# One attention tile moves from the second half of a gated FFN kernel to its attention stage, the rest start one chunk later, and the transfers at the change of halves are placed in another order

## The chip, the cores and the metric

The kernel runs on one core of a Trainium2 chip. The metric is device time in microseconds (us), the median of several executions. A profile, taken by the hardware profiler on one further execution, shows what each engine did: PE (TensorE, matrix products; its weight loads are listed as PEld), DVE (VectorE), ACT (ScalarE), POOL (GpSimd) and SP (SyncE, which here issues every transfer between the chip's memory and the on-chip buffers).

## What is computed

For 2048 tokens `x` of width 576 (all in float32):

```python
xn = layernorm(x)
q, k, v = split(xn @ wqkv)             # 32 heads of 18
pq, pk = phi(q), phi(k)                # phi(t) = (t + 1 if t > 0 else exp(t)) + 1e-6
kv = einsum("hsd,hse->hde", pk, v);  z = sum_s pk
o  = (pq @ kv) / (pq . z + 1e-6)       # linear attention, no softmax
s  = o @ wo
h  = gelu(xn @ w1 + b1)                # 576 -> 4608
g  = silu(h @ w2 + b2)                 # 4608 -> 576
out = x + s * g
```

## The kernel before, in words

Every float32 operand of a matrix product is split into a high and a low part, and a product is three matrix instructions (high by high, high by low, low by high). The two large products of the FFN are made with a seven-product scheme for 2 by 2 blocks of a matrix; the products of one block are numbered 1 to 7, and in the second matrix product they run in the order 1, 2, 7, 4, 5, 3, 6 (`ORDER`).

The work has four stages.

1. **Projections.** `q`, `k`, `v` of 16 token tiles of 128, the state `kv` and the sums `z`. Some tiles of `q` are written to the chip's memory (`q_dram`).
2. **Attention stage** (from `fold_wo` to `ordered.close()`). The masked state is folded with `wo` into five blocks `kw`, each split into high and low (`split_kw`, line 1191) and also stored (`store_kw`, line 1196, tensor `kw_dram`). Then, for each tile in the list `TO` (line 1065, nine tiles), GpSimd multiplies `q` by the sums (`by_sums`, line 1099, tile `bs`), VectorE makes the denominators (`denominators`, line 1106, tile `den`), GpSimd divides (`p_mult`, line 1114, tiles `vb` and `pbuf`, three buffers), ScalarE fills a pad (`pad`), TensorE transposes five blocks (`transpose_p`, line 1248; line 1252 in the profile, tile `ptp`), ScalarE and VectorE split the result (`th`, `tl`, lines 1256 to 1258), and TensorE makes 28 products into `ps_s` (`attend_mm`, line 1287). The result goes to `s_dram`. All engines' instructions here, SP's too, stay in the order of the program text (`in_order()`). `load_q(j)` (line 1178) reads a tile of `q` back; four buffers hold such tiles, and one becomes free when `p_mult` has read it.
3. **FFN in two halves of eight tiles**, 18 chunks of the loop at line 2050, numbered 0 to 17 here (`step` in the code; `c` counts within a half, so chunk 9 is `c == 0` of the second half). A chunk is 14 products of the first matrix product (profile line 1569, outputs `a`, `b`, `zy`, `e`, seven instructions each), then 14 half-products of the second one (line 1731, output `pm`, twelve instructions each). Around these, everything else is hung on a plan: `add(place, function)` puts work at one of 28 places of a chunk (`NS = 28`; places 0 to 13 are the first matrix product, 14 to 27 the second), and `at_step` writes it out there. The instructions of PE, DVE, ACT and POOL keep that order; the order on SP's queue is not fixed by hand. In the first half the split operands of `w1` and `w2` are made and stored; in the second half they are read back: `load_we` (line 1338, tile `we`), `W1Loaded` (line 1407, tiles `wa`, `wc`, `wd`), `load_six` (line 1420, `we<-op` in the profile), and `W2.load` (line 1658, tiles `w__...`, three buffers in turn, so that product 4's operand takes the buffer of product 1's).
4. **Tail**: chunk 17 without the seven-product scheme, and the last eight tiles of output.

At the change of halves, between chunks 8 and 9, the first half's four sums (`C11`, `C22`, `C21`, `C12`) are passed through silu and stored by `store_first` (line 1809, `c_dram<-macc`), to be gated and written out tile by tile in chunks 10 to 17. The tiles of attention that are not in `TO` (`LATER_TILES`, tiles 0 to 6) are done in the second half, one per chunk, by the class `Attention` (line 1927): its folded blocks come from `kw_dram` (`load_block`, `split_folded`, tile `kw`), the sums from `zb_dram` into `b2b` (`load_sums`), a tile of `q` into `qa`; the stations of one tile are in the table `A_AT`, by place relative to the next chunk (`load` 8 places ahead, `sums` 1 ahead, `transpose` at 4, `product` at 6). So a tile planned in chunk n is multiplied in chunk n + 1; tile 0 is planned in chunk 9.

```python
    A_AT = dict(
        load=-8, phi=-5, phi_max=-4, sums=-1, denominators=1, scale=1, pad=2, banks=3, transpose=4,
        operands=4, product=6, store=7,
    )
    W2_NEXT = {1: 24, 2: 26, 7: 27, 4: 44, 5: 46, 3: 48, 6: 50}
```

Of the kernel before, what the change touches and what calls it, by code (L numbers as in the profile page):

```python
# [30 lines left out]
NC = NF // CF  # L31
# [4 lines left out]
QH = 4  # L36
# [11 lines left out]
def linear_attention_gated_ffn(ctx, tc, x, xT, wqkv, wo, w1, w1e, b1, w2, b2, out):  # L48
# [804 lines left out]
    late = {}  # L853
# [206 lines left out]
    for p in range(2, NPR):  # L1060
# [3 lines left out]

    TO = [
        2 * NPR - 3, 2 * NPR - 4, 2 * QH, 2 * QH + 1, 2 * NPR - 2, 2 * QH + 2, 2 * NPR - 1,
        2 * QH + 3, 2 * QH - 1,
    ]
    NA = len(TO)
    kvz, sums_k, last_row, zb_first = (late[n] for n in ("kvz", "sums_k", "last_row", "zb"))  # L1070
# [120 lines left out]
    def split_kw(k, elo):  # L1191
        h, l = (w[k] for w in kw_ops)
        nc.scalar.copy(h, krs[k])
        elo.tensor_tensor(l, krs[k], h.bitcast(F32), op=SUB)
# [33 lines left out]
    def load_x_pair(q, p):  # L1228
        nc.sync.dma_start(X[:, q].bitcast(F32), x_dram[p])
# [18 lines left out]
    def transpose_p(j):  # L1248
        pb = p_bufs[j % len(p_bufs)]
        pt = bank2(f"ptp{j}").rearrange("p a b -> p (a b)")  # L1250
        for k in range(KT):
            nc.tensor.transpose(pt[:, k * P : (k + 1) * P], pb[:, k * P : (k + 1) * P], ident)
        th = thp.tile([P, KT, P], F32R, tag="th", name=f"th{j}")
        tl = thp.tile([P, KT - 1, P], F32R, tag="tl", name=f"tl{j}")
        p3 = pt[:, : KT * P].rearrange("p (k c) -> p k c", k=KT)
        nc.scalar.copy(th, p3)
        nc.vector.tensor_tensor(tl, p3[:, :4, :], th[:, :4, :].bitcast(F32), op=SUB)
        nc.vector.tensor_tensor(th[64:, 4, :], p3[64:, 4, :], th[64:, 4, :].bitcast(F32), op=SUB)
        pT[j] = (th, tl)

    split_kw(3, dve)
    store_kw(3)
    transpose_p(0)
    split_kw(4, dve)
    store_kw(4)
    load_x_pair(2, QH)
# [242 lines left out]
    for j in range(NA):  # L1509
        attend(j)  # L1510
        if j + 2 < NA:
            transpose_p(j + 2)
        if j + 3 < NA:
            pad(j + 3)
        if j == 0:
            phi_q_hi(TO[6])
        if j == 1:
            phi_q_max(TO[6])
        if j + 5 < NA:
            by_sums(j + 5)  # L1520
        if j + 4 < NA:
            denominators(j + 4)
            p_mult(j + 4)
        if j == 0:
            load_q(8)
            load_x_pair(3, QH + 1)
        beside(j)
    ordered.close()
    ph2.close()
# [11 lines left out]
    C11, C12, C21, C22, U1 = range(5)  # L1541
# [348 lines left out]
    NS = 28  # L1890
# [159 lines left out]
    for step in range(n_chunks):  # L2050
        half, c = divmod(step, NC)
        base = step * NS
        plain = step == n_chunks - 1
        h = HOps(c)
        if half == 1 and c == 0:
            a = Attention(None)
            add(base + 20, a.folded_places)
            add(base + 26, a.load_sums)
            for k in range(KT):
                add(base + 20 + k, a.load_block, k)  # L2060
                add(base + 26 + k, a.split_folded, k)
        if half == 1 and c < len(LATER_TILES):
            a = Attention(LATER_TILES[c])
            for what, at in A_AT.items():
                if what not in ("phi", "phi_max") or a.t < 4:
                    late = c == 0 and what in ("sums", "denominators", "scale", "pad")
                    add(base + NS + at + late, getattr(a, what))
        if half == 0:
            plan_w1(add, w1t[2 * step + 1], base, **P1)
            add(base, w2t[step].sum7)  # L2070
            for k in range(2):
                add(base + 2, w2t[step].sum4, k)
            for i, (at, lo) in PW2.items():
                add(base + at, w2t[step].hi, i)
                add(base + lo, w2t[step].lo, i)
            if (c, 5) not in w2_dram:
                w = w2t[step]
                for i, (at, hi, lo) in W2_SUMS_HERE.items():
                    add(base + at, w.sum5 if i == 5 else w.sum6)
                    add(base + hi, w.hi, i)  # L2080
                    add(base + lo, w.lo, i)
        change = step == NC - 1
        if not plain:
            add(base + (11 if change else 7), load_we, 2 * step + 2)
            add(base + (16 if change else 14), load_we, 2 * step + 3)
        if half == 0 and c < NC - 1:
            add(base + 0, make, W1, w1t, 2 * step + 2)
            add(base + 4, make, W1, w1t, 2 * step + 3)
            add(base + 1, lambda n=2 * step + 2, base=base: plan_w1(add, w1t[n], base, **P0))
            make(W2, w2t, step + 1)  # L2090
            add(base + 22, w2t[step + 1].load_raw)
            if (c + 1, 5) in w2_dram:
                for i, at in W2_SUMS_NEXT.items():
                    add(base + at, lambda i=i, n=step + 1: w2t[n].load(i))
        elif not plain:
            at = (11, 11, 16) if change else (7, 14, 24) if step == NC else (7, 14, 14)
            add(base + at[0], make, W1Loaded, w1t, 2 * step + 2)
            add(base + at[1], load_six, 2 * step + 2)
            add(base + at[2], make, W1Loaded, w1t, 2 * step + 3)
            if step + 2 < n_chunks:  # L2100
                make(W2, w2t, step + 1)
                for i, at in W2_NEXT.items():
                    add(base + max(at, 28 * change), lambda i=i, n=step + 1: w2t[n].load(i))
            else:
                make(W2, w2t, step + 1)

                w = w2t[step + 1]
                add(base + 13, w.load_raw)
                for f in range(CF):
                    add(base + 22 + f, lambda f=f, w=w: (w.plain(f), w.hi(("p", f))))  # L2110
                    add(base + 24 + f, w.lo, ("p", f))
        if not plain:
            if half == 0 and c == NC - 1:
                for k, at in X_AT.items():
                    add(base + at, load_x_next, k)
                add(base + 25, silu_first, C11)
                for k in range(2):
                    add(base + 26 + k, combine, C12, nc.vector, slice(2 * k, 2 * k + 2))
                    add(base + 26 + k, combine, C21, nc.gpsimd, slice(2 * k, 2 * k + 2))
            for what in ("S", "hi", "lo"):  # L2120
                for (i, pr), at in PH[what].items():
                    add(base + at, getattr(h, what), i, pr)
        if half == 1 and c == 0:
            add(base, silu_first, C12)
            add(base, silu_first, C21)
            add(base, combine, C22, nc.vector, slice(0, 2))
            add(base + 1, combine, C22, nc.vector, slice(2, 4))
            add(base + 1, silu_first, C22)
            for k, m in enumerate((C11, C22, C21, C12)):
                add(base + 5 + 2 * k, store_first, m)  # L2130
        if half == 1 and c:
            for k in range(2):
                tiles = {}
                def load(k=k, t=c - 1, tiles=tiles):
                    tiles[0] = finish_tiles(k)
                    finish_load(t, k, tiles[0])
                add(base, load)
                add(base + 4, lambda k=k, t=c - 1, tiles=tiles: finish(t, k, tiles[0]))
        if plain:
            for m in (C12, C21, C22):  # L2140
                add(base + 4, combine, m, nc.gpsimd)
            for t, at in enumerate((6, 7, 12, 13, 5, 13, 13, 13)):
                add(base + at, load_xs, t)
            for b, f, at, lo in (
                (0, 0, 7, 8), (0, 1, 8, 9), (1, 0, 10, 10), (1, 1, 10, 11), (0, 2, 11, 12),
                (0, 3, 12, 13), (1, 3, 13, 13), (1, 2, 13, 13),
            ):
                add(base + at, tail_split, b, f)
                add(base + lo, tail_lo, b, f)
        for j in range(CF // 2):  # L2150
            n = 2 * step + j
            u = Up(n, w1t.pop(n), xs)
            for k, i in enumerate(UP):
                u.step(i)
                h.add(j, u.g)
                at_step(base + 7 * j + k)
        if plain:
            break
        held = {}
        for k, i in enumerate(ORDER):  # L2160
            for q2 in (0, 2):
                product(c, i, q2, [h.ops[i, 0], h.ops[i, 1]], w2t[step].ops[i], held)
                at_step(base + 14 + 2 * k + q2 // 2)
        if change:
            second_half()
# [60 lines left out]
```

## Time and profile before

| | us |
|---|---|
| median of 3 runs | 1109.28 (1109.06 to 1110.73) |
| the profiled execution | 1107.14 |
| its span, first to last instruction | 1105.3 |

| engine | busy us | share of the span |
|---|---|---|
| PE | 1084.6 | 98% |
| PEld | 995.6 | 90% |
| DVE | 823.4 | 74% |
| ACT | 524.8 | 47% |
| POOL | 510.4 | 46% |

The transfers move 258.63 MB, 234 GB/s on average. A row of the windows view gives the stretch in us from the span's start, its length, the busy time and the number of instructions (x) of each engine in the order PE, PEld, DVE, ACT, POOL, then the granted clock of PE as a share of full speed, the busy share of the 16 DMA engines (it can come out a little over 1) and GB/s. A row of a timeline or of the chain has the start, the length, the engine with its line, and what is written and read; "q" after an engine's name is its queue of issues, and an arrow in brackets says what ended the idle time before it. A row of the waits view ends with the total in us, the number of times and the longest. A matrix instruction's shown length reaches past the start of the next one, so rates are read from starts.

### The profile page before, as it was taken

What the parts mean: (1) busy time and instruction counts of PE and PEld (TensorE: products, weight loads), DVE (VectorE), ACT (ScalarE), POOL (GpSimd) and SP (SyncE); (2) the same over time, 40 slices, a digit from 0 to 9 for tenths busy, and PEclk for the clock granted to TensorE, in tenths of its full rate; (3) what the DMA queues carried; (4) which work ended last, traced back from release to release, by engine and by line L of the source; (5) the groups of instructions that cost most, each with busy time, mean ns of one, the idle gap of its engine ahead of it and who ended that gap; (6) DMA issues with size and microseconds to landing.
All of it is one profiled execution on the core that took longest, in us unless ns stands there. A gap on an engine that the chain in (4) does not pass through costs nothing.

```text
span 1105.3 us, 17915 instructions
## 1 busy us (share of the span) xinstructions
PE 1084.6 (98%) x6492; PEld 995.6 (90%) x6492; DVE 823.4 (74%) x1207; ACT 524.8 (47%) x872; POOL 510.4 (46%) x536
## 2 busy tenths in 40 slices
PE   8999999999999999999999998999999999999998
PEld 7999999798998989989889897889989899999988
DVE  7997853768898898988989886665748475664856
ACT  7666665536454454554544543433524424242442
POOL 3133231458567595674866724243334435252340
PEclk9999999999999999999999999999999999999999
DMA  6778633899668577685685899776767677576753
GB/s 235 191 288 225 230 125 125 273 319 365 231 208 313 188 254 275 200 304 198 228 287 210 279 309 365 262 227 193 222 212 229 200 209 224 185 237 208 232 157 137
DMA packets 91184, 258.63 MB, mean 234 GB/s; under 512 B 12246, under 2 KB 25558, under 8 KB 88792
## 3 DMA queue, kind: packets, MB, share of 16 engines
q1 hardware_dynamic: 91096, 257.49, 70.4%
q8 instruction: 51, 0.84, 0.3%
q14 instruction: 37, 0.30, 0.1%
HBM read 155.16 MB, written 101.40 MB: 232 GB/s over the span
## 4 chain that ended last, share of the span: by engine, by line
PE 91%; DMA 3%; DVE 2%; ACT 2%; issue 1%; POOL 1%; SPq 0%; ACTq 0%; DVEq 0%; POOLq 0%
PE pm L1731 33%; PE e L1569 10%; PE zy L1569 10%; PE a L1569 10%; PE b L1569 5%; PE xaall L390 4%; PE x L390 3%; PE psa L1287 2%; PE pd L1852 2%; PE x1all L390 2%; PE ps_s L1287 2%; PE ps_kva L473 1%; PE x0all L390 1%; PE xakv L390 1%; DMA w__7431<-op 1%
## 5 line engine op out<-in xcount | busy, mean ns | idle before, releaser
L1668 POOL TENSOR_TENSOR g<-g 128x256 f32<-128x256 f32 x204 | 185.3, 938 | 60.3 <-DVE h_l L1329 53.4
L1737 DVE TENSOR_TENSOR macc<-pm,macc 128x576 f32<-128x576 f32 x218 | 163.7, 751 | 48.4 <-PE pm L1731 47.8
L1326 ACT CAST h_h<-g 128x512 fp32r<-128x512 f32 x204 | 122.7, 621 | 127.5 <-PE pm L1731 126.4
L1329 DVE TENSOR_TENSOR h_l<-g,h_h 128x512 fp32r<-128x512 f32 x204 | 165.5, 818 | 2.4 <-ACT h_h L1326 2.4
L1569 PE MATMUL a<-X,wa 128*128 128x512 f32 x432 | 110.1, 390 | 0.0
L1569 PEld LDWEIGHTS a<-X,wa 128*128 128x128 f32 x432 | 79.7, 188 | 15.2
L1586 ACT COPY mid<-a 128x512 f32<-128x512 f32 x36 | 21.1, 585 | 115.5 <-PE a L1569 115.5
L1589 DVE TENSOR_TENSOR mid<-b,mid 128x512 f32<-128x512 f32 x36 | 24.8, 689 | 65.1 <-PE b L1569 65.0
L1668 POOL TENSOR_TENSOR mid<-g 128x256 f32<-128x256 f32 x68 | 52.1, 786 | 45.7 <-ACT g L1577 44.6
L1377 POOL TENSOR_TENSOR w1raw<-w1raw 128x256 f32<-128x256 f32 x18 | 13.3, 740 | 116.4 <-ACT h_h L1326 71.6
L1569 PE MATMUL e<-X,wc 128*128 128x512 f32 x216 | 56.7, 399 | 0.0
L1577 ACT ACTIVATE g<-b,b1c 128x512 f32<-128x512 f32 x36 | 24.8, 689 | 65.6 <-DVE b L1595 65.6
L1569 PE MATMUL zy<-X,wd 128*128 128x512 f32 x216 | 54.9, 389 | 0.0
L1569 PE MATMUL zy<-X,wc 128*128 128x512 f32 x216 | 54.8, 389 | 0.0
L1569 PE MATMUL e<-X,wd 128*128 128x512 f32 x216 | 54.8, 389 | 0.0
L274 POOL TENSOR_TENSOR R<-R,bc 128x640 f32<-128x640 f32 x9 | 15.5, 1738 | 72.5 <-DMA R<-xT 49.1
L1569 PEld LDWEIGHTS zy<-X,wd 128*128 128x128 f32 x216 | 40.6, 188 | 8.6
L1569 PEld LDWEIGHTS e<-X,wc 128*128 128x128 f32 x216 | 40.8, 192 | 8.3
L1569 PEld LDWEIGHTS e<-X,wd 128*128 128x128 f32 x216 | 40.5, 188 | 8.4
L1569 PEld LDWEIGHTS zy<-X,wc 128*128 128x128 f32 x216 | 40.5, 188 | 8.4
L1577 ACT ACTIVATE g<-e,b1c 128x512 f32<-128x512 f32 x36 | 24.8, 689 | 46.3 <-DVE e L1602 46.3
L1984 POOL TENSOR_TENSOR qa<-qa,dena 128x576 f32<-128x576 f32 x7 | 8.2, 1169 | 79.8 <-issue 75.3
(1018 smaller groups left out, 3223.0 us busy)
## 6 DMA issues: line engine op xcount, KB each, us to landing
we<-we_dram SPq DMA_DIRECT2D x72, 224.0 KB
w2raw<-w SPq DMA_DIRECT2D x10, 1152.0 KB
x_dram<-X SPq DMA_DIRECT2D x6, 1792.0 KB
w1raw<-w SPq DMA_DIRECT2D x18, 512.0 KB
op_a<-wa SPq DMA_DIRECT2D x18, 512.0 KB
op_c<-wc SPq DMA_DIRECT2D x18, 512.0 KB
op_d<-wd SPq DMA_DIRECT2D x18, 512.0 KB
wc<-op_c SPq DMA_DIRECT2D x18, 512.0 KB
```

What stands on the lines that cost most here:

```text
L390: nc.tensor.matmul(dst, st, w, start=start, stop=stop, skip_group_check=True)
L1287: nc.tensor.matmul(ps[:, h, :HD], st[:, k, :], w[v][k][:, h * HD : (h + 1) * HD], start=(i == 0), stop=(i == len(seq) - 1),)
L1326: nc.scalar.copy(pair[0], src)
L1329: eng.tensor_tensor(pair[1], src, pair[0].bitcast(F32), op=SUB)
L1569: nc.tensor.matmul(ps, st, mv, start=first and n == 0, stop=n == len(seq) - 1, skip_group_check=True,)
L1577: nc.scalar.activation(g, ps, AF.Gelu_apprx_tanh, bias=b1c[:, f : f + 1])
L1586: nc.scalar.copy(m1_sb, A)
L1589: tt(u1_sb, B, m1_sb, op=ADD)
L1668: nc.gpsimd.tensor_tensor(dst[:, cs], a[:, cs], b[:, cs], op=op)
L1731: nc.tensor.matmul(ps[:, q, :HD], hs[p][st][:, cs], m[:, p, :], start=(n == 0 and i not in CHAIN), stop=(n == 5), skip_group_check=True,)
L1737: nc.vector.tensor_tensor(dst, src, dst, op=ADD)
L1852: nc.tensor.matmul(ps, st[:, cs], w_all.rearrange("p n d -> p (n d)")[:, w], start=(i == 0), stop=(i == len(seq) - 1),)
```

## The change

- `TO` has a tenth tile, tile 6 (`2 * QH - 2`), and its `q` is loaded at `j == 1` of the attention loop. `LATER_TILES` is thereby tiles 0 to 5.
- In the attention stage `transpose_p(0)` stands ahead of `split_kw(3)` and `store_kw(3)`.
- The later tiles are planned from chunk 10 on, so that the first is multiplied in chunk 11 (the second half's third chunk). The folded blocks and the sums are loaded in chunk 10 instead of chunk 9: the sums at place 0, the blocks at places 17 to 21, their splits at 23 to 27 (before: 26, 20 to 24, 26 to 30 of chunk 9). The special case of one place more for the first tile (`late`) goes.
- In chunk 9 the loads of `we` for chunk 10 stand at places 18 and 24 (before 7 and 14), `load_six` at 20 (before 14), and the store of `C12` at 17 (before 11).

```diff
     TO = [
         2 * NPR - 3, 2 * NPR - 4, 2 * QH, 2 * QH + 1, 2 * NPR - 2, 2 * QH + 2, 2 * NPR - 1,
-        2 * QH + 3, 2 * QH - 1,
+        2 * QH + 3, 2 * QH - 1, 2 * QH - 2,
     ]
...
+    transpose_p(0)
     split_kw(3, dve)
     store_kw(3)
-    transpose_p(0)
     split_kw(4, dve)
...
             load_x_pair(3, QH + 1)
+        if j == 1:
+            load_q(9)
         beside(j)
...
-        if half == 1 and c == 0:
+        if half == 1 and c == 1:
             a = Attention(None)
-            add(base + 20, a.folded_places)
-            add(base + 26, a.load_sums)
+            add(base, a.folded_places)
+            add(base, a.load_sums)
             for k in range(KT):
-                add(base + 20 + k, a.load_block, k)
-                add(base + 26 + k, a.split_folded, k)
-        if half == 1 and c < len(LATER_TILES):
-            a = Attention(LATER_TILES[c])
+                add(base + 17 + k, a.load_block, k)
+                add(base + 23 + k, a.split_folded, k)
+        if half == 1 and 0 < c <= len(LATER_TILES):
+            a = Attention(LATER_TILES[c - 1])
             for what, at in A_AT.items():
                 if what not in ("phi", "phi_max") or a.t < 4:
-                    late = c == 0 and what in ("sums", "denominators", "scale", "pad")
-                    add(base + NS + at + late, getattr(a, what))
+                    add(base + NS + at, getattr(a, what))
...
         if not plain:
-            add(base + (11 if change else 7), load_we, 2 * step + 2)
-            add(base + (16 if change else 14), load_we, 2 * step + 3)
+            for k, at in enumerate((11, 16) if change else (18, 24) if step == NC else (7, 14)):
+                add(base + at, load_we, 2 * step + 2 + k)
...
-            at = (11, 11, 16) if change else (7, 14, 24) if step == NC else (7, 14, 14)
+            at = (11, 11, 16) if change else (7, 20, 24) if step == NC else (7, 14, 14)
...
-            for k, m in enumerate((C11, C22, C21, C12)):
-                add(base + 5 + 2 * k, store_first, m)
+            for m, at in ((C11, 5), (C22, 7), (C21, 9), (C12, 17)):
+                add(base + at, store_first, m)
```

## The prediction

> **What bounds the kernel now.** The page says PE 98% busy, so the question is where the missing 2% sits and what the move does there. I read the windows view with one window per chunk; the bounds are the starts of each chunk's first product in the chain. Rows for chunks 8, 9, 10, 11 and 14:
>
> ```profile
> 608.74:653.72 44.98, 44.97 (x267) 40.83 (x267) 39.34 (x51) 22.77 (x37) 25.80 (x25) 1.00 0.93 298
> 653.72:703.13 49.41, 46.20 (x267) 42.14 (x266) 32.58 (x43) 23.46 (x34) 16.60 (x18) 0.97 0.99 332
> 703.13:757.12 53.99, 51.13 (x302) 46.40 (x301) 34.34 (x49) 22.18 (x35) 20.54 (x23) 0.97 0.72 219
> 757.12:806.10 48.98, 48.98 (x301) 45.01 (x300) 30.48 (x44) 20.35 (x32) 19.12 (x22) 1.00 0.72 220
> ...
> 904.84:954.05 49.21, 49.21 (x301) 45.01 (x300) 30.43 (x43) 15.95 (x27) 19.56 (x22) 1.00 0.69 213
> ```
>
> A plain chunk takes 44.98 us with PE never idle; one with an attention tile 48.98 to 49.21. Chunk 9 has no tile and takes 49.41; chunk 10 has one and takes 53.99. Both show PE idle and a clock of 0.97. Second, PE's waits from 660 to 760 us, and third the chain there:
>
> ```profile
> PE pm L1731 <- DMA w__7431<-op: 3.2, 1, 3.2
> PE pta L1996 <- POOL qa L1984: 2.0, 1, 2.0
> PE pm L1731 <- DMA w__7961<-op: 0.9, 1, 0.9
> ```
> ```profile
> 675.96 3.20 PE pm L1731 x24
> 679.18 9.44 DMA w__7431<-op
> ...
> 713.23 1.30 PE pta L1996 x5
> 714.53 2.67 PE e L1569 x7
> ...
> 736.86 7.10 DMA w__7961<-op
> ...
> 765.09 0.55 PE pta L1996 x5
> 765.63 1.62 PE e L1569 x7
> ```
>
> In chunk 9, product 4's operand (`w__7431`) is issued at 679.18, as soon as product 1 has freed its buffer, and lands 9.44 us later; PE reaches it after products 2 and 7 (6.4 us, two times 3.20) and waits 3.2. In chunk 10 the first tile's transposes wait 2.0 us for POOL, and then five transposes take 1.30 instead of 0.55 and the next product 2.67 instead of 1.62. Fourth, the granted clock just behind the two long waits:
>
> ```profile
> 689.41:692.82 3.41, 3.41 (x16) 3.41 (x15) 1.36 (x2) 0.00 (x0) 0.00 (x0) 0.50 0.87 320
> 713.30:716.71 3.41, 3.41 (x11) 2.93 (x12) 0.99 (x2) 1.44 (x3) 3.00 (x4) 0.50 0.28 101
> ```
>
> Each of these waits was followed by 3.41 us at half clock, worth 1.7 us on top (a half of 3.41). It is all that chunk 10's mean of 0.97 holds (1.7 / 53.99 = 0.03), so its 0.9 us wait had no such stretch. The chain is PE nearly everywhere else from 250 us on, so time is to be had only in these two chunks and in the attention stage.
>
> **The change, part by part.** *Chunk 9.* What stands on SP's queue ahead of `w__7431`, and the sizes:
>
> ```profile
> 662.09 0.57 SPq L1811 DMA_DIRECT2D c_dram<-macc  x1
> 664.88 1.18 SPq L1346 DMA_DIRECT2D we<-we_dram  x2
> ...
> 669.41 5.45 SPq L1811 DMA_DIRECT2D c_dram<-macc  x3
> 675.99 1.18 SPq L1346 DMA_DIRECT2D we<-we_dram  x2
> 677.23 1.07 SPq L1425 DMA_DIRECT2D we<-op  x2
> 679.18 0.32 SPq L1661 DMA_DIRECT2D w__7431<-op  x1
> ```
> ```profile
> c_dram<-macc SPq DMA_DIRECT2D x4, 576.0 KB
> we<-we_dram SPq DMA_DIRECT2D x4, 224.0 KB
> we<-op SPq DMA_DIRECT2D x2, 256.0 KB
> kw<-kw_dram SPq DMA_DIRECT2D x1, 288.0 KB
> ```
>
> The DMA engines are full (0.99, 332 GB/s), so a transfer's landing is set by the bytes ahead of it. The new places put four `we` loads, the two of `load_six` and the store of `C12` behind product 4's load: 4 x 224 + 2 x 256 + 576 = 1984 KB, at 332 GB/s 6.1 us. The load needs to be 3.2 us earlier. It cannot be issued earlier, and 9.44 - 6.1 = 3.3 us would be its landing; with the queue still partly filled, as for `w__7961`, 7.1. Needed are about 6.3: a wait of 0 to 0.8 is left. I take 0, the nearer end, since the loads of this stage get shorter by more than the 3.2 that is needed; with the wait the half clock goes: 49.41 to 44.98, **-4.4** (3.2 and 1.7 make 4.9, but the chunk lost 4.4, and that is what can come back). Next late would be products 5, 3 and 6, whose loads now share the queue with the moved ones; each has again some 6.4 us from free buffer to use, and the stage also loses the five `kw` blocks, the sums and a `qa` (7 x 288 KB), all issued in it until now. The moved loads themselves are first used in chunk 10, nine places or more after their own; at 44.98 / 28 = 1.6 us a place that is 14 us, against a landing of 9.44 in the full queue. The store of `C12` must land before product 3 adds to that sum, at place 24, seven places or 11 us later.
>
> *Chunk 10.* The tile leaves: 53.99 less its work (49.2 - 44.98 = 4.2), the POOL wait 2.0 and its half clock 1.7. What stays is the wait for `w__7961`, 0.9. So 44.98 + 0.9 = 45.9, **-8.1**. Added are the sums and five `kw` blocks, 1728 KB. The chunk moves 219 GB/s where chunk 9 moved 332, so there is room for (332 - 219) x 54 us = 6 MB. Cost 0 if they travel ahead of the products; if they fall between the loads of products 4, 5, 3 and 6, up to one wait like that of `w__7431`, 4.4 with its half clock. I take 0: SP's queue doesn't follow the places strictly. In chunk 10 a load of place 20 went ahead of one of place 14:
>
> ```profile
> 727.52 0.32 SPq L1954 DMA_DIRECT2D qa<-q_dram  x1
> 730.26 0.32 SPq L1418 DMA_DIRECT2D wa<-op_a  x1
> ```
>
> The splits of `kw` (5 ACT and 5 DVE instructions) move with them; both engines are under 70% busy there, and PE does not wait for them in chunk 9 today. The first tile, in chunk 11, finds its sums loaded half a chunk before; it then meets the conditions of the tile that chunk 11 does today without a wait. Chunks 11 to 16 keep one tile each: 0.
>
> *Attention stage.* The tenth tile costs what a late tile costs, transposes and 28 products:
>
> ```profile
> 231.84 0.55 PE ptp L1252 x5
> 232.39 3.72 PE ps_s L1287 x28
> ```
>
> **+4.3**. Its `q` can be issued when `p_mult(5)` has freed a buffer, at 226.2 (the row of 224.71 in the last fence of this part); even with 9.44 us to landing it is there at 235.6, and its transposes come after those of tile 8, past 244. SP keeps the program's order here, so the stores of `ps_s` behind that issue wait for the same buffer, about a microsecond; nobody needs them before the second half. POOL's two instructions for it delay the `w1` sums behind them by some 4 us, about as much as the FFN starts later.
>
> The moved `transpose_p(0)` stands before a split that waits for a transfer:
>
> ```profile
> 204.60 0.67 ACT L1193 CAST kw_h<-kr 128x576 fp32r<-128x576 f32 x1 [2.28 <-DMA kr<-kw]
> 205.18 0.69 ACT L1256 CAST th<-ptp 128x640 fp32r<-128x640 f32 x1
> ```
> ```profile
> 203.30 1.25 PE L1252 MATMUL ptp<-ident,vb 128*128 128x128 f32 x10
> 205.91 0.52 PE L1287 MATMUL ps_s<-kw_h,th 128*128 128x288 f32 x2 [1.36 <-ACT th L1256]
> ...
> 212.07 0.80 PE L1252 MATMUL ptp<-ident,pbuf 128*128 128x128 f32 x5
> ...
> 221.82 0.77 PE L1252 MATMUL ptp<-ident,vb 128*128 128x128 f32 x5 [0.83 <-POOL vb L1116]
> ...
> 227.89 0.50 PE L1287 MATMUL ps_s<-kw_h,th 128*128 128x288 f32 x2 [0.89 <-DVE th L1258]
> ```
> ```profile
> 218.77 1.43 POOL L1101 TENSOR_TENSOR bs<-q,zb 128x576 f32<-128x576 f32 x1 [2.31 <-DMA q<-q_dram]
> ...
> 224.71 1.47 POOL L1116 TENSOR_TENSOR pbuf<-q,den 128x576 f32<-128x576 f32 x1 [0.57 <-DVE den L1112]
> ```
>
> ACT's `th` can start at about 204.05 instead of 205.18, and PE's first products 1.1 us earlier. But the tile at 221.82 hangs on a `q` that lands at 218.77 whatever PE does, so nothing before it counts; what can be won is the 0.89 of the wait at 227.89, whose DVE chain starts some 0.55 to 0.9 earlier. **-0.7**. Against it stand gaps that open ahead of slower neighbours: PE would start tile 0 near 204.8, finish it 3.9 later at 208.7, and find POOL's next tile, which it takes today at 212.07, perhaps 0.7 earlier at 211.4: a gap of 2.7 us, longer than the 2.0 that was followed by half clock. That loss (1.7) is hidden by the wait at 221.82. If the clock stays up there, tile 2 ends near 219.9 and the gap before 221.82 is 1.9; a half clock after that one isn't hidden. So this edit lies between -0.9 and +1.0.
>
> **Sum:** -4.4 - 8.1 + 4.3 - 0.7 = -8.9. The profiled execution would go from 1107.14 (span 1105.3, 1.8 around it) to 1098.2. The median of the runs is 1109.28, 2.1 above the profiled one, and I take the difference from it: **1100.4**.
>
> The Trainium skill's page "TensorE: Matmul & The Clock Gate", section "Part 1: The HAM clock gate", says that the clock falls to half after at least one idle window of about 3.4 us. By that rule neither wait, of 3.2 and of 2.0 us, would lower the clock, and the half-clock stretches would not go with the waits; the sum would be 3.4 us smaller. The rows of 0.50 stand right behind both waits, so I go by them and give the other reading a small chance below.
>
> **The rivals.**
> - *The half clock isn't the waits' doing* but comes in these chunks anyway. Then 2 x 1.7 stays: -8.9 + 3.4 = -5.5, 1103.8. For it: the two waits differ by 1.2 us and brought the same 3.41 us. Against: both stretches begin within 0.7 us of a wait's end, and chunks without a long wait show 1.00. Chance 0.04. (It is where the rule of the Trainium skill's page "TensorE: Matmul & The Clock Gate" would lead.)
> - *The order in SP's queue stays much as it was*, since ready loads go ahead of waiting ones (the 727.52 row): `C12`, `load_six` and one pair of `we` again ahead of product 4's load. Then only the other pair of `we` goes, 448 KB or 1.4 us; of the wait 1.8 remains, near enough to 2.0 to count its half clock: 1.8 + 1.7 = 3.5 come back, 1103.9. Against: in chunk 9, where the queue is full, the issues (662.09 to 679.18) did follow the places. Chance 0.15.
> - *The wait moves to chunk 10*: `kw` loads between those of products 4 to 6. -8.9 + 4.4 = -4.5, 1104.8. For: program places 17 to 21 lie there. Against: the room in the DMA, the 727.52 row. Chance 0.11.
> - *Slower than before:* ACT and DVE take their instructions in order, and `kw`'s splits now stand at places 23 to 27, among the casts for products 3 and 6. A block loaded at 17 has six places, 9.7 us, to land, just over the longest landing in the rows above (9.44). Beyond that each us holds ACT, and through the casts PE, 1 us. To end over the old time it takes 8.9 + 2.2 = 11.1 us more, landings above 21 us: 1112 and up. No row here is near that. Chance 0.05.
>
> **How the numbers follow.** The forecast, all three parts, has 0.6, between 1098.5 and 1102.5 (rests of 0.8, the reordering's +1.0); 0.05 is for what I haven't seen. Range 1097.5 to 1105.5: it takes in the first three rivals and leaves out the slower one and gains over 11.8. A difference of 0.2% (2.2 us) is about what a measurement of this kernel can tell from none. Faster by more: the forecast, the first three rivals less a little, 0.88; within: 0.05; slower: 0.07.
>
> **What would show it.** Right: chunk 9 near 45.0 and chunk 10 near 45 to 46 with a clock of 1.00, no wait for product 4's operand over 1 us, no `pta` in chunk 10; `ps_s` x280, and the FFN's first product some 3.6 us later than today. Wrong: a half clock in chunks 9 to 11, a `w__` wait over 2 us, `kw` waits on ACT, or an FFN that starts over 6 us later.

## The result, and the profile after

The changed kernel takes **1102.13 us** in the median of nine runs (1099.64 to 1108.96), the kernel before 1109.20 in nine runs beside it (1105.48 to 1110.73). The ratio is 0.9948 with a 95% interval of 0.9926 to 0.9969: a gain of 7.1 us in the medians. The profiled execution took 1101.58, its span 1099.8, so between the two profiled executions 5.5 us are gone. (The same kernel, run once more beside the kernel before in a later set, came to 0.9966, a gain of 3.3 us in the medians; see `after_again` below. The 7.1 is the larger of two measurements.)

The attention stage of the kernel before:

```profile
203.30:248.65 45.35, 41.56 (x299) 39.95 (x298) 31.36 (x55) 20.11 (x38) 22.92 (x18) 0.96 1.00 331
```

The windows view of the changed kernel, in the same columns as before; the rows are the attention stage, chunk 9, chunk 10, and all from chunk 11 to the end:

```profile
202.87:251.50 48.63, 43.80 (x333) 42.72 (x332) 33.21 (x60) 21.86 (x41) 26.04 (x20) 1.00 1.02 339
656.54:703.89 47.35, 45.42 (x269) 40.77 (x267) 31.52 (x42) 19.10 (x28) 16.76 (x18) 1.00 0.98 305
703.89:750.64 46.75, 45.38 (x269) 41.02 (x268) 29.27 (x41) 20.77 (x33) 17.32 (x21) 1.00 0.84 298
750.64:1099.80 349.16, 342.86 (x2084) 314.01 (x2083) 218.85 (x314) 130.21 (x210) 127.97 (x140) 1.00 0.67 202
```

| | before | after | moved | forecast |
|---|---|---|---|---|
| attention stage | 45.35 | 48.63 | +3.3 | +3.6 |
| chunk 9 | 49.41 | 47.35 | -2.1 | -4.4 |
| chunk 10 | 53.99 | 46.75 | -7.2 | -8.1 |
| chunk 11 to the end | 348.2 | 349.2 | +1.0 | 0 |

(The 348.2 is the span 1105.3 less chunk 11's start, 757.12. The attention stage also begins 0.4 earlier: 202.87 for 203.30.) The clock is 1.00 in each of the four rows, where the attention stage had 0.96 and chunks 9 and 10 had 0.97. The stage's half clock before, at 208.13, cost it nothing that can be seen: in `order_only` below, which leaves the stage as it was, the stage took 45.89 with the clock up. Chunks 9 and 10 still take 2.4 and 1.8 us more than a plain chunk's 44.98. PE's waits from 640 us on (what it waited for, then us in total, times, and the longest) say what for:

```profile
PE pm L1733 <- ACT h_h L1326: 2.5, 3, 1.2
PE pm L1733 <- DMA w__7514<-op: 1.0, 1, 1.0
PE pm L1733 <- DMA w__7598<-op: 0.7, 1, 0.7
PE pm L1733 <- DVE h_l L1329: 0.2, 1, 0.2
PE a L1571 <- DMA wa<-op_a: 0.2, 1, 0.2
```

The 3.2 us wait for product 4's operand, POOL's 2.0 and the 0.9 of chunk 10 are all gone. New are waits for the operands of products 5 (`w__7514`) and 6 (`w__7598`) in chunk 9, and for a cast of ScalarE, `h_h`; its longest, 1.2, lies in chunk 10, the other 1.3 in later chunks.

SP's queue in chunk 9 (start, length, what is issued) shows where the first two come from:

```profile
670.48 1.96 SPq L1813 DMA_DIRECT2D c_dram<-macc  x2
682.60 0.33 SPq L1663 DMA_DIRECT2D w__7474<-op  x1
682.98 1.27 SPq L1813 DMA_DIRECT2D c_dram<-macc  x1
685.79 0.33 SPq L1663 DMA_DIRECT2D w__7514<-op  x1
686.17 1.36 SPq L1346 DMA_DIRECT2D we<-we_dram  x2
688.99 0.33 SPq L1663 DMA_DIRECT2D w__7558<-op  x1
689.36 0.92 SPq L1425 DMA_DIRECT2D we<-op  x2
692.24 0.32 SPq L1663 DMA_DIRECT2D w__7598<-op  x1
```

Between 672.4 and 682.60 nothing is issued: product 4's load waits for its buffer, and all that was moved stands behind it. Then the moved transfers come one by one between the loads of products 4, 5, 3 and 6. Over most of the pause the DMA engines still worked off what had been issued before. In a window of 4 us around its end they were busy 0.44 of the time:

```profile
679.50:683.50 4.00, 4.00 (x33) 4.00 (x32) 2.89 (x6) 2.19 (x4) 3.19 (x5) 1.00 0.44 148
```

So the transfers were put off past a stretch in which the memory had little to do, into one in which PE waits for them. ScalarE's timeline in chunk 10 shows the third wait:

```profile
739.68 0.67 ACT L1948 CAST kw<-kw 128x576 fp32r<-128x576 f32 x1
743.07 0.69 ACT L1963 ACTIVATE ea<-qa 128x576 f32<-128x576 f32 x1 [2.72 <-DMA qa<-q_dram]
743.77 1.28 ACT L1964 ACT_TABLE_LOAD   x1
...
746.47 0.60 ACT L1326 CAST h_h<-g 128x512 fp32r<-128x512 f32 x1
```

Line 1963 is `phi` of the first late tile. Its `q`, loaded only three places before, lands late; ScalarE stands for 2.72 us, and the cast that PE wants is behind it.

### The profile page after: what moved, and what is told of

It is laid out like the page before. It is cut to its first block, busy times and chain, and to the rows that moved or that the text cites. A ratio compares the mean times of both kernels' runs of the same rounds, so it can differ in the third digit from the quotient of the medians.

```text
span 1099.8 us, 17916 instructions
## 1 busy us (share of the span) xinstructions
PE 1080.0 (98%) x6492; PEld 990.8 (90%) x6492; DVE 824.0 (75%) x1207; ACT 524.9 (48%) x872; POOL 512.3 (47%) x536
## 4 chain that ended last, share of the span: by engine, by line
PE 91%; DMA 5%; ACT 2%; issue 1%; DVE 1%; POOL 1%; SPq 0%; ACTq 0%; POOLq 0%; DVEq 0%
PE pm L1733 33%; PE a L1571 10%; PE e L1571 10%; PE zy L1571 10%; PE b L1571 5%; PE xaall L390 4%; PE x L390 3%; PE ps_s L1287 2%; PE pd L1854 2%; PE x1all L390 2%; PE psa L1287 2%; DMA X<-x_dram 2%; PE ps_kva L473 1%; PE x0all L390 1%; PE xakv L390 1%; DMA wa<-op_a 1%
## 5 line engine op out<-in xcount | busy, mean ns | idle before, releaser
L1329 DVE TENSOR_TENSOR h_l<-mid,h_h 128x512 fp32r<-128x512 f32 x34 | 36.0, 1060 | 1.2
```

What stands on the lines that cost most here:

```text
L1329: eng.tensor_tensor(pair[1], src, pair[0].bitcast(F32), op=SUB)
```

## The experiments

**Theory:** the gain has two sources that need each other, the tiles' later start (which frees chunk 10) and the transfers' order (which frees product 4's operand); what the forecast has and the result lacks is lost to the empty stretch of SP's queue and to the late `q`. **Rivals:** the tile that moves is itself the gain; the order alone is; the remaining waits are simply the price of the loads that moved to chunk 10. The ratios below are to the kernel before on the same chip, with 95% intervals. Most of these intervals overlap each other, so the experiments are read from the stages, of one profiled execution each.

### One part undone or done alone

`order_old` is the changed kernel with chunk 9's transfers at their old places:

```diff
-for k, at in enumerate((11, 16) if change else (18, 24) if step == NC else (7, 14)):
+for k, at in enumerate((11, 16) if change else (7, 14)):
-at = (11, 11, 16) if change else (7, 20, 24) if step == NC else (7, 14, 14)
+at = (11, 11, 16) if change else (7, 14, 24) if step == NC else (7, 14, 14)
-for m, at in ((C11, 5), (C22, 7), (C21, 9), (C12, 17)):
+for m, at in ((C11, 5), (C22, 7), (C21, 9), (C12, 11)):
```

> The changed kernel with the loads and stores of chunk 9 back at their old places (we at 7 and 14, load_six at 14, the store of C12 at 11); tile 6 and the late tiles stay moved. Theory A (the order of the queue is what took product 4's wait away): chunk 9 takes about 49.4 us again, with a wait of some 3 us for product 4's operand and, if waits bring it, a half clock behind it; chunk 10 about 46.5; the time 2 us above the changed kernel, 1103 to 1105. Theory B (the kw blocks, sums and qa that left chunk 9 made the room): chunk 9 stays near 47.4 and product 4 doesn't wait over 1 us.

Measured: 1103.76, ratio 0.9972 (0.9951 to 0.9994). Its chunks 9 and 10, and PE's first two waits there:

```profile
657.70:707.65 49.95, 46.75 (x268) 41.88 (x267) 31.50 (x42) 19.09 (x28) 16.73 (x18) 0.97 1.01 332
707.65:753.18 45.53, 44.84 (x268) 40.79 (x267) 29.96 (x41) 20.68 (x33) 18.02 (x21) 1.00 0.83 257
```
```profile
PE a L1571 <- DMA wa<-op_a: 1.9, 1, 1.9
PE pm L1733 <- DMA w__7484<-op: 1.3, 1, 1.3
```

In the old order product 4 waits again (`w__7484` is its operand here), but 1.3 us and not the 3 that were expected, and the 2.6 us by which chunk 9 is longer than after are mostly something else: a wait of 1.9 for `wa` in the first matrix product, and a half clock behind it, from 672.33 to 675.74, worth 1.7. That wait comes and goes from profile to profile (see "Still open"). The half clock also makes PE late for product 4, which probably hides part of the wait there: `tile_only` below, where SP's queue is the same up to product 4's load and `wa` is late too, but no half clock follows, waits the full 3.2. So the stage shows that without the new order product 4 still waits, and not how much the order is worth; by the time, `order_old` can't be told from the changed kernel (0.9968 for `transpose_old` in the same set).

Chunk 10 is 1.2 shorter than after, and the reason is a second difference that the edit brought along. With the old places SP also issued the loads for the late tiles earlier, the first `kw` already in chunk 9 and the `q` 14 us sooner than after (736.74):

```profile
702.28 0.43 SPq L1943 DMA_DIRECT2D kw<-kw_dram  x1
...
722.77 0.45 SPq L1956 DMA_DIRECT2D qa<-q_dram  x1
```

The wait for the cast behind `phi` is gone here. So `order_old` is not a clean removal of one part, since the order on SP's queue doesn't follow the places strictly.

`order_only` is the kernel before with the new order in chunk 9, the tiles left as they were (the diff above the other way round).

> The kernel before with only chunk 9's loads and stores at the new places; seven late tiles, kw blocks still loaded in chunk 9. Theory A: product 4 doesn't wait, but kw, qa and the moved loads now queue among the loads of products 5, 3 and 6, and these wait 2 to 3 us in all: chunk 9 at 47.5 to 48.5. Chunk 10 keeps its wait for POOL (about 54). The time 1 to 2 us under the kernel before, 1107.5. Theory B: chunk 9 stays near 49.4, no gain.

Measured: 1110.60, ratio 1.0036 (1.0009 to 1.0063): no gain, rather a small loss.

```profile
653.94:704.60 50.66, 45.68 (x269) 40.83 (x267) 32.01 (x44) 23.54 (x34) 16.71 (x18) 1.00 0.98 310
704.60:760.31 55.71, 51.68 (x301) 46.75 (x300) 33.80 (x49) 22.19 (x35) 20.48 (x23) 0.94 0.75 238
```
```profile
PE pta L1996 <- POOL qa L1984: 4.0, 1, 4.0
PE a L1569 <- DMA wa<-op_a: 2.7, 1, 2.7
PE pm L1731 <- DMA w__7551<-op: 1.6, 1, 1.6
PE pm L1731 <- DMA w__7461<-op: 0.5, 1, 0.5
```

Product 4 (`w__7421` here) doesn't wait any more. But products 5 (`w__7461`) and 6 (`w__7551`) now wait 0.5 and 1.6, and the first late tile, still due in chunk 10, is later than before: the wait for POOL goes from 2.0 to 4.0, with 6.8 us at half clock from its second half on. Chunk 9 has the wait for `wa` again, 2.7, without which it would be shorter than before. Without the tiles' later start the order mostly hands the wait on.

`tile_only` is the kernel before with tile 6 in the attention stage and six late tiles, which start in chunk 10 as before; no other edit.

```diff
-        2 * QH + 3, 2 * QH - 1,
+        2 * QH + 3, 2 * QH - 1, 2 * QH - 2,
...
+        if j == 1:
+            load_q(9)
```

> The kernel before with tile 6 in the attention stage, and nothing else: six late tiles, the first still multiplied in chunk 10, so that chunk 16 has none. Theory A (a tile costs the same 4.2 us in either place, and the gain came from where the second half lost it): attention stage 45.35 + 4.3 = 49.6 us, chunk 16 at 45.0 instead of 49.2, chunks 9 and 10 as before (49.4 and 54.0): no difference, 1109. Rival (a tile is cheaper in the attention stage): a stage under 48.5 and a time under 1107.

Measured: 1105.88, ratio 0.9990 (0.9970 to 1.0009). Its attention stage, chunk 9, chunk 10 and the chunk that lost its tile:

```profile
202.36:251.94 49.58, 44.19 (x333) 42.67 (x331) 34.39 (x60) 21.82 (x41) 25.88 (x20) 1.00 1.00 331
657.04:710.78 53.74, 48.04 (x269) 43.13 (x267) 32.73 (x44) 23.56 (x34) 16.74 (x18) 0.94 0.95 313
710.78:761.42 50.64, 49.19 (x302) 44.91 (x300) 33.79 (x49) 22.18 (x35) 20.56 (x23) 1.00 0.76 237
1010.28:1055.04 44.76, 44.76 (x269) 40.80 (x267) 29.86 (x41) 16.88 (x28) 17.20 (x21) 1.00 0.70 206
```

The stage pays 4.2 (49.58 for 45.35) and chunk 16, now at 44.76, gives back what a tile costs. Moving a tile gains nothing that can be measured; the rival falls. Chunks 9 and 10 were expected unchanged (49.4 and 54.0) and were not: chunk 9 has a wait of 2.5 for `wa`, the old 3.2 for product 4 and 6.8 us at half clock from the end of that on, and chunk 10 has a shorter wait for POOL, 1.5, without a half clock. This profile is the slowest of its ten executions (1109.83). What the later start adds is seen in chunk 10, which has no tile then: 46.75 after and 45.53 in `order_old`, for 50.64 here. The ratios of `order_old` and `tile_only`, 0.9972 and 0.9990, have intervals that overlap. So one half of the theory is shown, that the order gains nothing without the later start; that the later start needs the order is not.

`transpose_old` is the changed kernel with `transpose_p(0)` behind `split_kw(3)` and `store_kw(3)` again.

> The changed kernel with transpose_p(0) behind split_kw(3) and store_kw(3) again. Theory A (the earlier transposes take away the wait at tile 4 of the stage, 0.9 us, and nothing else counts because tile 4 hangs on a q that lands at its time): the stage from the first transposes to the first FFN product takes 49.5 instead of 48.6, the rest is the same; time 1 us above the changed kernel. Rival (no part of it reaches the end): 48.6.

Measured: 1102.99, ratio 0.9968 (0.9950 to 0.9986); the attention stage took 49.02, with PE's 0.9 wait for DVE's `th` back. The stage took 48.6 to 48.8 in the executions with the edit whose clock stayed up there. But `tile_only`, whose stage differs from the changed kernel's in this edit alone, took 49.58. So the edit is worth between 0.2 and 1.0 us in the stage, which the time of the kernel can't tell from nothing. The 0.9 wait is not reliably gone either: `queue_filled`, `qa_kw_early`, `qa_early` and `filled_qa` have the edit and show 0.8 or 0.9 of it, with a shorter wait for POOL's `vb` (0.2 to 1.7) than the changed kernel's 2.5.

### The two new waits

`after_again` is the changed kernel once more, as a measure beside the next three.

> The changed kernel once more, as the control of this set. Ratio to the kernel before 0.993 to 0.997; chunks 9 and 10 at 47 to 48 and 46 to 49 us, with small waits of product 4 to 6 operands and of a cast in chunk 10; attention stage 48.5 to 49, or 1.7 more with a half clock. If half clocks come at another place or not at all, they depend on where the waits fall in time and not on the waits' length alone.

Measured: 1102.77, ratio 0.9966 (0.9944 to 0.9987); chunk 9 47.56, chunk 10 46.47, but the attention stage 50.01 with a stretch at half clock (last section).

`queue_filled` is the changed kernel with the store of `C12` at place 11 and the first pair of `we` at 14, so that SP has them to issue before it comes to product 4's load; the second pair and `load_six` stay behind it.

```diff
-enumerate((11, 16) if change else (18, 24) if step == NC else (7, 14))
+enumerate((11, 16) if change else (14, 24) if step == NC else (7, 14))
-((C11, 5), (C22, 7), (C21, 9), (C12, 17))
+((C11, 5), (C22, 7), (C21, 9), (C12, 11))
```

> The changed kernel with C12's store back at place 11 and the first pair of we at 14; load_six stays at 20, the second pair at 24. Theory A (the queue stands idle some 4 us ahead of product 4's load, since SP waits there for its buffer, and what was moved behind it now delays products 5 and 6): about 1 MB goes into that idle time, product 4 still doesn't wait, the waits for products 5 and 6 (1.0 and 0.7) go, chunk 9 takes 45 to 46 where the first product's operand isn't late; 1 to 1.5 us under the control. Rival (any byte ahead delays product 4): a wait of 1 us or more for product 4.

Measured: 1100.99, ratio 0.9955 (0.9933 to 0.9977). Its chunks 9 and 10, and the same 4 us as above:

```profile
658.05:702.78 44.73, 44.73 (x269) 40.72 (x267) 31.51 (x42) 19.10 (x28) 16.75 (x18) 1.00 0.98 322
702.78:751.06 48.28, 46.90 (x269) 42.39 (x267) 30.60 (x42) 20.78 (x33) 18.02 (x21) 0.96 0.86 289
```
```profile
679.50:683.50 4.00, 4.00 (x29) 3.83 (x28) 3.13 (x5) 2.00 (x3) 3.19 (x5) 1.00 1.08 374
```

Chunk 9 takes 44.73, PE never idle, and product 4 doesn't wait although only 224 x 2 + 256 x 2 = 960 KB were kept behind its load, not 1984. At 332 GB/s that is 3.0 us of the 3.2 that were missing. That the empty stretch was the cause rests on more than this one profile: of the three with these places (this one, `both`, `filled_qa`) none has a wait for the operand of any product in chunk 9, and each of the five with the changed kernel's places has one, from 0.2 us in all (`transpose_old`) to 1.7 (`after`). Chunk 10 keeps its 1.2 us wait for `h_h`, here with a half clock behind it. The time can't be told from that of `after_again`.

`qa_kw_early` is the changed kernel with the five `kw` loads at places 2 to 6 of chunk 10 (17 to 21) and the first late tile's `q` at place 2 (20):

```diff
-                add(base + 17 + k, a.load_block, k)
+                add(base + 2 + k, a.load_block, k)
...
-                    add(base + NS + at, getattr(a, what))
+                    add(base + (2 if what == "load" and c == 1 else NS + at), getattr(a, what))
```

> The changed kernel with the five kw loads of chunk 10 at places 2 to 6 instead of 17 to 21 and the first late tile's q at place 2 instead of 20. Theory A (ScalarE's phi waits for a q that lands behind the kw loads and holds the casts queued behind it): the waits for ACT h_h in chunk 10, 2.5 us in all, go and chunk 10 takes 45.0 to 45.5 instead of 46.6; 1 to 1.5 us under the control. Rival (the casts are late because of POOL or of the weights): chunk 10 stays at 46.5.

Measured: 1106.63, ratio 1.0013 (0.9994 to 1.0033): the whole gain is lost.

```profile
705.25:754.32 49.07, 46.36 (x269) 42.30 (x267) 30.23 (x41) 20.76 (x33) 18.01 (x21) 0.97 0.81 282
```
```profile
PE pm L1733 <- DMA w__7949<-op: 2.7, 1, 2.7
...
PE pm L1733 <- ACT h_h L1326: 0.2, 1, 0.2
```

The wait for `h_h` behind `phi` goes (all waits for `h_h` fall from 2.5 to 0.2), but six transfers of 288 KB stand ahead of the others of the chunk, and product 4's operand (`w__7949`) is 2.7 us late. The six push `load_six` from 719.16 to 728.88, right ahead of that operand's load. That seems to be what costs, since in `order_old` four of the five `kw` loads went out as early, with `load_six` at 721.92, and product 4's operand held PE by no wait of its own (0.7 at product 4 is put on a cast); no run tests it. `both`, the last two edits together, shows the same late operand.

> Both edits together. Theory A: 2 to 3 us under the changed kernel, ratio to the kernel before about 0.992; chunks 9 and 10 both under 46 us where no operand of the first products is late. Rival (the bytes only change places): as the changed kernel.

Measured: 1103.70, ratio 0.9993 (0.9970 to 1.0015): chunk 9 46.36, of which 1.4 is a wait for `wa`, and chunk 10 49.80 with 3.4 for `w__7949`.

That leaves one transfer to move instead of six: the `q` alone to place 2, the `kw` loads left where they are. `qa_early` does it in the changed kernel, `filled_qa` in `queue_filled`.

> The changed kernel with one edit: the first late tile's q is loaded at place 2 of chunk 10 instead of place 20; the folded blocks kw stay at places 17 to 21. Theory A (ACT's phi of the first tile waits for qa, behind it stand casts that PE waits for): the waits of PE for ACT's h_h in chunk 10, 2.5 us in the changed kernel's profile, fall to 0.2 or less as they did with kw and qa moved together, and since one load of 288 KB is moved and not six, product 4's operand is no longer late (there 2.7 us and a half clock): chunk 10 44.9 to 45.6 instead of 46.5 to 46.8, ratio against the changed kernel's own about 0.999, against the kernel before about 0.9945 to 0.996. Rival B (the casts wait for kw, not for qa): h_h waits of 1 to 2.5 us stay, chunk 10 stays at 46.5. Rival C (any transfer put ahead of product 4's operand is paid for there): a wait for a w__79 operand of 1 us or more, chunk 10 at 47 or over.

Measured: 1101.72, ratio 0.9955 (0.9933 to 0.9978); chunk 10 45.51. Its one wait is another one than that behind `phi`:

```profile
737.14 0.50 PE L1733 MATMUL pm<-w__7944,h_h 128*128 128x288 f32 x2 [0.67 <-ACT h_h L1326]
```

It stands at the first instruction of product 4, and `phi` runs only at 741.69, without waiting for `q`. What held PE there stays open. (The expectation had put all 2.5 us of the changed kernel's waits for `h_h` in chunk 10; only 1.2 lay there.) A longer chunk 11 (50.03) and chunk 9 (48.28, of it 1.6 idle in the first matrix product) hide the gain in the time.

> Chunk 9 as in the version with its idle queue filled (store of C12 back at place 11, first pair of we at 14, second at 24, load_six at 20) and the first tile's q at place 2 of chunk 10. If the two effects add (theory A): chunk 9 at 44.7 to 45.5 without a wait over 0.7 us for products 5 and 6, chunk 10 at 44.9 to 45.6 without a wait for h_h, profiled span 1.5 to 3 us under the 1099.05 of the filled version, ratio 0.992 to 0.9945. Rival C (a transfer ahead of product 4's operand in chunk 10 is paid for): chunk 10 at 47 to 49 with a wait for a w__79 operand and a half clock, ratio 0.996 or more. Rival D (the attention stage's half clock, which comes or not by execution, covers the difference): ratio within 0.002 of 0.9955 whatever chunk 10 does.

Measured, in six executions: **1099.11, ratio 0.9934** (0.9909 to 0.9959), the lowest of all. Chunks 9 and 10, and PE's waits from 600 us on that lie in them:

```profile
656.37:705.13 48.76, 45.23 (x269) 40.65 (x267) 31.51 (x42) 19.09 (x28) 16.75 (x18) 1.00 0.94 314
705.13:749.80 44.67, 44.67 (x268) 40.79 (x267) 29.97 (x41) 20.68 (x33) 18.05 (x21) 1.00 0.87 294
```
```profile
PE a L1571 <- DMA wa<-op_a: 2.1, 1, 2.1
...
PE zy L1571 <- DMA X<-x_dram: 1.4, 1, 1.4
```

Chunk 10 takes 44.67 without a wait. The late `q` is shown as the cause of the wait behind `phi`: it is there in the four profiles that issue the `q` late (`after`, `after_again`, `transpose_old`, `queue_filled`, 0.9 to 1.2) and in none of the five that issue it early (`order_old`, `qa_kw_early`, `both`, `qa_early`, `filled_qa`). In its second half chunk 9 has no wait either; the forecast's 44.98, and the 44.7 to 45.5 expected here, were missed by the two waits in the first half, for `X` and `wa`. By stages both edits do what they should. By the time, the interval overlaps those of the changed kernel and of `qa_early`, so the step from 1102 to 1099 is likely and not settled.

## Why the prediction was right, and where it was off

The forecast was 1100.4, 8.9 us less than before; measured are 1102.13 and a ratio whose whole interval lies under 1. The mechanism was right in the main, and the term for chunk 9 was too large. Some of the nearness is luck: the profiles have 5.5 us of the 8.9, the nine runs 7.1, and the second measurement of the same pair 3.3.

- **What bounds the kernel, and where.** Right. The loss sat in chunks 9 and 10, and the waits named there are gone.
- **Attention stage, +4.3 - 0.7.** Right: +3.3, and `tile_only` shows +4.2 for the tile. The FFN starts 2.9 us later (251.50 for 248.65; forecast 3.6). The bound above, a half clock that isn't hidden, came true in other executions: `order_old`, `after_again` and `both` took 50.0 to 50.4 in this stage, 1.4 or more on top. The other one, which a later wait hides, came in `qa_kw_early`, at 212.39, with a stage of 48.8. The 0.7 for the moved transposes lies within the 0.2 to 1.0 that the runs allow; the 0.9 wait that was to pay for it comes back in four of the profiles.
- **Chunk 9, -4.4.** The mis-sized term: -2.1. The step that failed is "next late would be products 5, 3 and 6 ... each has again some 6.4 us from free buffer to use". It took the 6.4 us for enough; the loads of 5 and 6 share the memory with the moved ones and were 1.0 and 0.7 late. It also moved 1984 KB where 960 do (at 332 GB/s, 3.0 us for the 3.2 that were missing), and did not ask what SP would issue in the 10 us before product 4's buffer is free. With that filled, the chunk gave the forecast in full: 49.41 to 44.73.
- **Chunk 10, -8.1.** Nearly right: -7.2. Tile, POOL's wait and half clock went; instead of the 0.9 for `w__7961` stands 1.2 for `h_h`. The slower rival had named the place (ScalarE in order, casts behind it) but the wrong transfer: `kw`'s splits cost nothing that can be seen, the `q` for `phi` did. In the kernel before, the same `phi` ran at 694.25 right behind its casts, 7.2 us after its `q` was issued. The likely reason is that PE's 3.2 us wait and half clock had made those casts later, so that a wait that goes uncovers one that it hid; no run tests this.
- **Chunks 11 to 16, 0.** Off by 1.0; 1.3 of the 2.5 us for `h_h` lie in later chunks.
- **The rivals.** In chunk 9 of the changed kernel SP's order did follow the places, so the second one is out; in `order_old` it didn't. The 0 for the five `kw` blocks was right for another reason than the one given: they did not travel ahead of the products, but went out between the loads of products 4, 5 and 3 (729.88 to 737.68), and no operand was late. The wait that "moves to chunk 10" is what `qa_kw_early` made, by loads that went early: 2.7 us and a half clock, about the 4.4 that was put on it. Its cause, loads between those of products 4 to 6, wasn't it.
- **The half clock.** It went with the waits in chunks 9 and 10, as forecast. But the rule behind it, that a wait of 2.0 us or more brings it, is too simple: the changed kernel's attention stage has waits of 2.1 and 2.5 us at a clock of 1.00, and the 1.2 us of `queue_filled` brought one.

**Still open:** the wait for `wa` in the first half of chunk 9. Between executions of one and the same kernel it was 0.2 and 1.1 (`after`, `after_again`), over all kernels 0 to 2.7. In the chain it follows the load of `X`, 14.46 us in `filled_qa`. It is no part of the change (the two kernels built on the kernel before, `order_only` and `tile_only`, have 2.7 and 2.5), but it alone makes chunk 9 uneven by over 2 us, sometimes with a half clock behind it, and nothing here tells what sets it. Differences of chunk 9 as a whole between these profiles mean little; the waits in its second half are the better measure.

## What to carry to other kernels

When a load is late behind others in a full queue, put off only as many bytes as its lateness needs (here 3.0 us' worth for 3.2), and look at what the queue does while the load waits for its buffer: what was ready should go out then, ahead of it. Move the one transfer that is waited for, not its whole group. And ask for every wait that goes which other wait it may have covered: here one late operand on ScalarE, which takes its instructions in the order of the plan, held the cast behind it, and PE with it.

## What was not expected of the hardware

**Half clock comes by a grid, not by the wait.** Away from the first and the last microseconds of a span, every half-clock stretch lasts 3.413 us or twice that, and in one execution all of them begin on one grid of that step: in the kernel before at 208.13, 689.41 and 713.30, which are 141 and 7 steps apart. The grid's place differs from execution to execution. (The changed kernel has no such stretch; its grid is carried back from 1097.61, where its clock falls at the end of the span, 257 steps after 220.38. In `after_again`, that last fall, at 1098.73, lies 257 steps after its stretch at 221.51.) What counts seems to be how much PE did in the 3.41 us of the grid just before. Three such windows that were followed by half clock, of the kernel before, `after_again` and `queue_filled`:

```profile
709.89:713.30 3.41, 1.42 (x7) 0.85 (x7) 2.50 (x6) 0.78 (x2) 1.28 (x2) 1.00 0.46 147
```
```profile
218.09:221.51 3.42, 1.01 (x9) 0.78 (x8) 3.22 (x7) 0.52 (x3) 3.42 (x3) 1.00 1.02 352
```
```profile
743.69:747.11 3.42, 2.04 (x12) 1.43 (x11) 0.95 (x2) 3.38 (x6) 0.00 (x0) 1.00 0.77 233
```

and two that were not, of the changed kernel and of `after_again`:

```profile
220.38:223.79 3.41, 1.75 (x14) 1.75 (x15) 3.34 (x5) 1.48 (x3) 3.41 (x3) 1.00 1.02 334
```
```profile
207.85:211.27 3.42, 1.55 (x12) 1.51 (x13) 1.71 (x4) 3.35 (x6) 1.49 (x2) 1.00 0.95 397
```

PE was busy 1.0 to 2.0 us in the first three and 1.6 and 1.8 in the others, so its busy time alone doesn't decide between 1.5 and 2.0. All windows of the grid from 190 to 1090 us, in the ten profiles that have a grid from such a stretch or fall (all but `qa_early` and `filled_qa`), say the same: of those at full clock with 1.9 us or more of idle PE all ten were followed by half clock, of those with 1.38 to 1.87 four in 25, and of those with less none. The changed kernel's 2.5 us wait, from 219.50 to 222.04, passed: the grid cut it in two, and the window that holds the greater part had 1.75 us of work, so it lay where the clock mostly stays up. In `after_again`, the same program, the grid lay so that the window had 1.0, and the clock fell; its stage took 50.01 for 48.63. So much the same wait costs 1.4 us more in one execution than in another; how much of the spread of the times this is was not tried.

The Trainium skill's page "TensorE: Matmul & The Clock Gate", section "Part 1: The HAM clock gate", tells of a free-running activity window, and the grid agrees with it in step and in that it runs on by itself. That it takes about one whole idle window (some 3.4 us) to fall to half, the traces here don't bear out: 1.4 us idle in a window, in `queue_filled`, was enough.
